# Turning the second expert place's rows by DMA transposes, in a gated-attention and expert-layer kernel

## The chip, the cores and the metric

The kernel runs on one core of a Trainium2 chip. The metric is the device time of one execution in microseconds. Three runs of the kernel before are shown; their median is 394.35 us. The engines of a core are called PE (matrix multiplications), DVE (vector), ACT (scalar), POOL (general) and SP (issues DMAs); 16 DMA engines move data for all of them.

## The reference

Two blocks follow each other. The first is a gated recurrent attention over sequences of 768 steps, the second a layer of 8 experts to which each of the 3072 rows is sent by the largest gate value.

```python
for t in range(S):                                   # 4 batches, 8 heads, width 48
    state = alpha[:, :, t, :, None] * state + np.einsum('bhd,bhe->bhde', k[:, :, t], v[:, :, t])
    y[:, :, t] = np.einsum('bhd,bhde->bhe', q[:, :, t], state)
x = y.transpose(0, 2, 1, 3).reshape(3072, 384)
logits = x @ w_gate                                  # (3072, 8)
expert_idx = np.argmax(logits, axis=1)
gate_w = softmax(logits)[row, expert_idx]
for e in range(8):
    rows = expert_idx == e
    out[rows] = gate_w[rows, None] * (np.maximum(x[rows] @ w1[e], 0.0) @ w2[e])
```

w1 is 384 x 1024 and w2 1024 x 384 for each expert, all in float32.

## The kernel before, in words

**Attention** takes the first 137 us or so. It works through 24 tiles of 128 rows, writes each row, scaled by its gate weight, to a buffer in DRAM (`x_d`), and finds out which rows go to which expert.

**Experts** follow as eight *places* (`groups`, `caps`). Place 0 is always expert 0, the others follow in order of how many rows an expert got. Place 1 has 416 rows, each later one 8 less. What does not fit is done by a loop after the places. For a place:

- `gather` (L372, POOL) fetches its rows from `x_d` by indirect DMAs, one for each block of 128 rows.
- The rows are *turned*, so that the width of 384 lies on the partitions: tile `xgT` (`g["xT"]`), one buffer.
- `row_sums` (DVE) makes five sums of halves of `xgT` in tile `t`, and `weight_sums` sums of halves of the weights in `s1` and `s2`. With these, places 1 to 7 do both layers by a scheme of seven products in place of eight (`chain`, `layer1`, `layer2`).
- The result `zT` is turned back and scattered to the output by POOL (`put`, L1078).

There are two ways to turn. `turn` (L855 on) has PE transpose each block of 128 x 128 against an identity into PSUM (L860), and DVE or ACT copy it to `xgT` (L861). `x_halves` (L866 on) splits a block of rows into its upper and lower 16-bit halves (L870, tile `xh`), has SP issue a DMA transpose for the block (L871, tile `xt`), and `x_whole` (L874 on) joins the halves to `xgT` on ACT (L878). Before the change, place 0 and place 1 are turned by `turn`, places 2 to 7 by the halves. Tile `xt` has one buffer, `xh` four.

**Place 0** is done in two parts. The 256 rows known early (`eg`) have layer one during the end of the attention, and layer two by `early_layer2` in two blocks j of 128 rows and eight pieces f (L1205, 2 matmul instructions to a piece). The *rest* of 168 rows is turned by `turn(g0)`, and then has `rest_layer1` (L1213 on): eight f, of which the even ones get their relu on ACT (L1228) and the odd ones on DVE (L1225). After each odd one a stretch of `places()` runs on DVE; that is the planning for the loop after the places, and it makes `xn`, which SP loads at L1343. `rest_layer2` (L1231 on) has three d of eight f (L1236), each with a copy to `zT` on ACT (L1239); its three results use the two banks of pair pA in turn.

**Order.** The program is written under a manual schedule (`tc.manual_schedule()`): each engine runs its instructions in the order of the program text, and an instruction that waits holds what stands behind it on its engine. So the generators (`l2`, `pl`, `between`) that are stepped with `next` are the order written out by hand. SP issues weight loads (`weights`, L179 and L182), the DMA transposes, and the writes of `x_d` in that order. Weights have two buffers for each layer, so `weights(i + 2, 1)` waits until place i has used its w1, while place 1's two loads find free buffers.

The order about the change, before it: layer two of early block 0 (eight pieces); gather of place 1; early block 1, pieces 0 to 3; `turn(g0)`; `rest_layer1`; early block 1, pieces 4 to 7, and its scatter; `weights(1, 2)`, `weights(2, 1)`; gather of place 2; the halves of place 2 on POOL; `turn(nxt)` of place 1 (first step of `turned()`); `ahead(1)`, the layer-one weight sums of place 1; `rest_layer2` d = 0; `row_sums` of place 1; d = 1 and 2; `weights(2, 2)`; then `layer1` of place 1 (L966).

Of the kernel before, what the change touches and what calls it, by code (L numbers as in the profile page):

```python
# [8 lines left out]
F32 = mybir.dt.float32  # L9
# [11 lines left out]
def kernel(  # L21
# [31 lines left out]
    C = 128  # L53
# [8 lines left out]
    DB = Dm // C  # L62
# [9 lines left out]
    NJ = 4  # L72
    SR = NJ * C
    CAP0, STEP = 424, 8
# [101 lines left out]
    def fetch(ex, layer):  # L176
        if layer == 1:
            w = wpool.tile([C, DB, F], F32, name="w1")
            nc.sync.dma_start(w[:], moe_w1[bass.ds(ex, 1)].rearrange("e (a p) f -> p (e a) f", p=C))  # L179
        else:  # L180
            w = wpool.tile([C, FB, Dm], F32, name="w2")
            nc.sync.dma_start(w[:], moe_w2[bass.ds(ex, 1)].rearrange("e (a p) d -> p (e a) d", p=C))  # L182
        return w
# [4 lines left out]
    FH = FB // 2  # L188
# [5 lines left out]
    def sub(eng, out, a, b):  # L194
        eng.tensor_tensor(out, a, b, op=ALU.subtract)  # L195
# [164 lines left out]
    def weights(i, layer):  # L360
        if 0 < i < E:
            ex = nc.sync.value_load(pd["xe"][0:1, i : i + 1], min_val=0, max_val=E - 1)
            groups[i][f"w{layer}"] = fetch(ex, layer)

    def blocks(g, by=1):
        return [(j, min(C, -(-(g["n"] - j * C) // by) * by)) for j in range(-(-g["n"] // C))]
# [22 lines left out]
    with tc.tile_pool(name="ld", bufs=6) as ld, \  # L389
         tc.tile_pool(name="work", bufs=2) as work:  # L390
        st = {s: {} for s in range(NT)}
        y = ps.tile([C, 2, 512], F32, name="y")
# [436 lines left out]
        _, s_e, gf_e, sf_e = next(d)  # L829
# [4 lines left out]
    wk = ctx.enter_context(tc.tile_pool(name="moe_wk", bufs=1))  # L834
# [4 lines left out]
    def bank(n):  # L839
        b = banks[n]  # L840
        if len(b) < 2:
            t = pairs[n][len(b)]
            if n == "y":
                b.append(y[:, t, :])
            else:
                b.append(ps.tile([C, 512], F32, name=t, bufs=2 if t == "tp" else 1)[:])
        else:
            b.append(b.pop(0))
        return b[-1]

    def blocks_of(t):
        return t[:, : DB * C].rearrange("p (a c) -> p a c", a=DB)


    def turn(g, *names):  # L855
        g["xT"] = wk.tile([C, DB, CAP0 + 8], F32, name="xgT")
        for j, r in blocks(g):
            tp = blocks_of(bank(names[j]))
            for a in range(DB):
                nc.tensor.transpose(tp[:, a, :r], g["xg"][:r, j, a * C : (a + 1) * C], ident[:r, :r])  # L860
            (nc.scalar.copy if j % 2 else nc.vector.tensor_copy)(g["xT"][:, :, j * C : j * C + r], tp[:, :, :r])  # L861
            if j == 1:
                yield

    def x_halves(g, copy=nc.scalar.copy):

        g["xt"] = wk.tile([C, NJ, 2 * DB, C], U16, name="xt")
        for j, r in blocks(g, 16):
            t = wk.tile([C, 2, Dm], U16, name="xh", bufs=4)
            copy(t[:r], g["xg"][:r, j, :].bitcast(U16).rearrange("p (c h) -> p h c", h=2))  # L870
            nc.sync.dma_start(g["xt"][:, j, :, :r], t[:r].rearrange("p h c -> p (h c)"), transpose=True)  # L871
            yield

    def x_whole(g):  # L874
        g["xT"] = wk.tile([C, DB, CAP0 + 8], F32, name="xgT")
        to = halves(g["xT"])
        for j, r in blocks(g):
            nc.scalar.copy(  # L878
                to[:, :, :, j * C : j * C + r], g["xt"][:, j].rearrange("p (h a) t -> p h a t", h=2)[:, :, :, :r],
            )  # L880

    def halves(t):
        return t.rearrange("p a t -> p (a t)").bitcast(U16).rearrange("p (a t h) -> p h a t", h=2, a=DB)

    def row_sums(g):
        m = g["n"] // 2
        g["t1"] = wk.tile([C, 5, CAP0 // 2 + 12], F32, name="t1")
        x, t = g["xT"], g["t1"][:, :, :m]
        h0, h1 = slice(0, m), slice(m, 2 * m)
        sub(nc.vector, t[:, 0], x[:, 0, h1], x[:, 0, h0])  # L890
        sub(nc.vector, t[:, 1], x[:, 1, h1], t[:, 0])
        sub(nc.vector, t[:, 2], x[:, 1, h1], x[:, 0, h1])
        sub(nc.vector, t[:, 3], x[:, 1, h0], t[:, 1])
        sub(nc.vector, t[:, 4], x[:, 2, h0], x[:, 2, h1])
# [305 lines left out]
    def early_layer2(j, fs):  # L1200

        if 0 in fs:
            eg["z"] = bank("y" if j else "pA")
        for f in fs:
            nc.tensor.matmul(  # L1205
                eg["z"][:, :Dm], lhsT=eg["h"][:, f, j * C : (j + 1) * C], rhs=groups[0]["w2"][:, f, :],
                start=(f == 0), stop=(f == FB - 1),
            )
        if FB - 1 in fs:
            yield  # L1210
            scatter(eg, j, C, eg["z"][:, :Dm])
        yield

    def rest_layer1(g, beside):
        n = g["n"]
        g["h"] = wk.tile([C, FB, CAP0], F32, name="h_sb")
        for f in range(FB):
            hp = bank("p" + "CBA"[f % 3])
            for a in range(DB):
                nc.tensor.matmul(  # L1220
                    hp[:, :n], lhsT=g["w1"][:, a, f * C : (f + 1) * C], rhs=g["xT"][:, a, :n],
                    start=(a == 0), stop=(a == DB - 1),
                )
            if f % 2:
                nc.vector.tensor_scalar_max(g["h"][:, f, :n], hp[:, :n], 0.0)  # L1225
                next(beside, None)
            else:
                nc.scalar.activation(g["h"][:, f, :n], hp[:, :n], AF.Relu)  # L1228

    def rest_layer2(g, d):  # L1230
        n = g["n"]  # L1231
# [12 lines left out]
    pl = places()  # L1244
# [2 lines left out]
        g["gi"], g["si"] = cols_of(gp, i * NJ), cols_of(sp, i * NJ)  # L1247
    gather(groups[1])
    next(l2)
    next(early_layer2(1, range(FH)))  # L1250
    for _ in turn(g0, "pC", "pC"):
        pass

    def beside(i):

        work = [z_halves(groups[i - 1])]
        if i == 1:
            work += [weight_sums(groups[1], 2, nc.vector)]
        while work:
            work = [w for w in work if next(w, w) is not w]  # L1260
            yield

    for i, g in enumerate(groups):
        nxt = groups[i + 1] if i + 1 < E else None
        rest = []

        last = i == E - 1

        def begin():
            if last:  # L1270
                rows_layer2(g, 0, ready)
            else:
                p1, tail = layer2(g)
                p1()
                rest.append(tail)

        if last:

            nc.gpsimd.drain()
        if i:  # L1280
            layer1(g, beside(i), begin, last)
        else:
            rest_layer1(g, pl)

            for _ in early_layer2(1, range(FH, FB)):
                pass
            weights(1, 2)
        weights(i + 2, 1)
        if i + 2 < E:
            gather(groups[i + 2])  # L1290
        if i == 0:
            for _ in x_halves(groups[2], nc.gpsimd.tensor_copy):
                pass

        def ahead(*layers):
            if nxt:
                for layer in layers:
                    for _ in weight_sums(nxt, layer, nc.vector):
                        pass

        def turned():
            if i == 0:
                for _ in turn(nxt, "pC", "pC", "y", "pB"):
                    pass
                yield
                row_sums(nxt)
                yield
            z_whole(groups[i - 1], nc.scalar.copy, 0, 1)
            yield
            if nxt:  # L1310
                row_sums(nxt)
            z_whole(groups[i - 1], nc.scalar.copy, 2)
            z_whole(groups[i - 1], nc.vector.tensor_copy, 3)
            yield
            if i + 2 < E:
                for _ in x_halves(groups[i + 2]):
                    pass
            yield

        between = turned()  # L1320

        if 0 < i < E - 1:
            x_whole(nxt)
        if last:
            for _ in between:
                pass
            for j, r in blocks(g):
                rows_layer2(g, j, (*([] if j == 0 else ready), FH - 1, FB - 1))
                scatter(g, j, r, g["z"][:r, :Dm], shared=j == NJ - 2)
        elif i:  # L1330
            rest[0](lambda: ahead(*((1,) if i == E - 2 else (1, 2))), between)
        else:
            next(between)
            ahead(1)
            rest_layer2(g, 0)
            next(between)
            rest_layer2(g, 1)
            rest_layer2(g, 2)
        weights(i + 2, 2)
# [4 lines left out]
    with tc.If(nx > 0):  # L1344
        with tc.For_i(0, nx, 1) as i:
# [13 lines left out]
            g = dict(n=C, w1=fetch(ex, 1), w2=fetch(ex, 2), gi=lambda j, r: gi[:, 0:1], si=lambda j, r: si[:, 0:1], apart=False)  # L1359
# [32 lines left out]
```

## Time and profile before

| | |
|---|---|
| three runs, median | 394.35 us |
| the profiled execution's own time | 394.27 us |
| its span, first to last instruction | 392.5 us |
| busy: PE / DVE / ACT / POOL | 382.1 / 211.6 / 225.5 / 149.7 us |
| mean granted clock of PE | 0.999 |
| rest's layer one, first matmul (L1220) | 156.91 us |
| rest's layer two, first matmul (L1236) | 167.91 us |
| place 1's layer one, first matmul (L966) | 174.85 us |

Times are in us from the first instruction of the profiled execution. In a timeline, a line has start, length, engine, line of the kernel, operation, output <- input, number of instructions merged, and in brackets how long the engine was idle ahead of it and what released it. The ends of matmuls are modelled, so that lengths of neighbours overlap; starts are the firmer figure. PEld are the weight loads of PE, which run beside its matmuls. SPq is the queue of SP: the length of a DMA there is the time that issuing took, and the time to landing is told apart from it.

### The profile page before, as it was taken

How to read it: one execution, taken by the hardware profiler on the slowest of the kernel's cores; microseconds unless marked ns; L12 is line 12 of the kernel's file. 1: busy time of each engine (PE TensorE's matmuls, PEld its weight loads, DVE VectorE, ACT ScalarE, POOL GpSimd, SP SyncE). 2: the span in 40 equal slices, each digit the busy share in tenths (PEclk: the TensorE clock that was granted, in tenths of full speed). 3: DMA queues.
4: the chain of work that ended last, by engine and by line, in shares of the span. 5: the costliest groups of instructions: out<-in, count | busy, mean ns of one | idle time of the engine just before them, and what ended most of it. 6: DMA issues, size and time to landing. Idle time of an engine off the chain costs nothing.

```text
span 392.5 us, 9105 instructions
## 1 busy us (share of the span) xinstructions
PE 382.1 (97%) x3390; PEld 325.6 (83%) x3390; DVE 211.6 (54%) x651; ACT 225.5 (57%) x515; POOL 149.7 (38%) x203
## 2 busy tenths in 40 slices
PE   6999999999999999999999999999999999999994
PEld 4678888888888785899889979979979979979852
DVE  5554667676675566455853572582581681552200
ACT  5476677777655441126664776675665765673540
POOL 6646564789768204184051034025026012021041
PEclk9999999999999999999999999999999999999999
DMA  9999998999996215768939659658668766600321
GB/s 172 204 182 231 189 223 188 226 201 220 236 224 178 96 42 216 256 227 236 158 137 260 77 202 206 177 187 216 169 200 193 187 201 150 172 21 36 60 72 42
DMA packets 153921, 67.44 MB, mean 172 GB/s; under 512 B 136715, under 2 KB 148098, under 8 KB 153876
## 3 DMA queue, kind: packets, MB, share of 16 engines
q1 hardware_dynamic: 148772, 57.13, 60.8%
q0 software_dynamic: 3408, 9.64, 8.0%
q8 instruction: 27, 0.44, 0.5%
q10 hardware_dynamic: 1696, 0.08, 0.3%
q14 instruction: 18, 0.15, 0.1%
HBM read 49.00 MB, written 9.58 MB: 149 GB/s over the span
## 4 chain that ended last, share of the span: by engine, by line
PE 78%; issue 15%; POOL 2%; ACT 2%; DVE 1%; DMA 1%; POOLq 0%; ACTq 0%; DVEq 0%
PE tp L1048 7%; PE tp L489 6%; PE sA L502 6%; PE y L539 5%; PE x L966 4%; PE sA L966 4%; PE x L576 4%; PE sA L1031 4%; PE tp L966 3%; PE sB L966 3%; PE cum L966 3%; PE x L1031 3%; PE y L529 3%; PE cum L430 2%; PE tp L1031 2%
## 5 line engine op out<-in xcount | busy, mean ns | idle before, releaser
L1078 POOL DMA_INDIRECT out_dram<-zo,sp x25 | 26.1, 1042 | 137.5 <-ACT zo L1103 127.0
L479 POOL TENSOR_TENSOR kqb<-k_sb,icp 128x384 f32<-128x384 f32 x23 | 23.0, 1001 | 29.6 <-PE y L550 12.4
L1048 PE MATMUL tp<-h_sb,w 128*128 128x416 f32 (+5 forms) x96 | 33.9, 496 | 0.0
L502 PE MATMUL sA<-qT,kT 48*128 48x128 f32 x192 | 27.7, 284 | 0.9 <-DVE qT L493 0.9
L372 POOL DMA_INDIRECT xg<-x_rows,gp x25 | 24.0, 962 | 10.0 <-issue 6.5
L502 PE MATMUL sB<-qT,kT 48*128 48x128 f32 x192 | 27.7, 285 | 0.0
L489 PE MATMUL tp<-ident,kqb 128*128 128x128 f32 x192 | 26.2, 279 | 0.6 <-DVE kqb L479 0.6
L1048 PEld LDWEIGHTS tp<-h_sb,w 128*128 128x128 f32 x96 | 18.0, 190 | 10.3 <-issue 3.7
L502 PEld LDWEIGHTS sA<-qT,kT 48*128 48x128 f32 x192 | 23.1, 187 | 3.8 <-ACT kT L495 1.1
L192 DVE TENSOR_TENSOR h_sb<-sB,u 128x208 f32<-128x208 f32 (+6 forms) x28 | 10.1, 360 | 27.3 <-PE sB L966 20.8
L977 ACT ACTIVATE h_sb<-h_sb 128x208 f32<-128x208 f32 (+6 forms) x28 | 10.2, 366 | 25.2 <-DVE h_sb L192 25.2
L479 POOL TENSOR_TENSOR kqb<-q_sb,cp 128x384 f32<-128x384 f32 x23 | 23.1, 1004 | 2.8 <-DMA q_sb<-in_q_dram 2.3
L192 DVE TENSOR_TENSOR h_sb<-cum,u 128x208 f32<-128x208 f32 (+6 forms) x28 | 10.1, 360 | 26.1 <-PE cum L966 18.7
L489 PEld LDWEIGHTS tp<-ident,kqb 128*128 128x128 f32 x192 | 20.5, 140 | 3.4 <-issue 1.2
L558 ACT COPY yT<-y 128x512 f32<-128x512 f32 x24 | 14.1, 587 | 16.0 <-PE y L550 10.3
L966 PE MATMUL tp<-xgT,w 128*128 128x208 f32 (+6 forms) x112 | 23.1, 329 | 0.0
L502 PEld LDWEIGHTS sB<-qT,kT 48*128 48x128 f32 x192 | 23.1, 187 | 0.0
L510 DVE TENSOR_TENSOR dA<-sA,cmask 128x512 f32<-128x512 f32 x24 | 16.5, 689 | 11.2 <-PE sB L502 11.0
L195 DVE TENSOR_TENSOR th<-h_sb,th 128x208 f32<-128x208 f32 (+5 forms) x48 | 17.4, 362 | 7.9 <-ACT h_sb L979 7.9
L576 PE MATMUL x<-iw,yT 128*64 128x104 f32 x368 | 20.8, 255 | 0.1
L1103 ACT COPY zo<-zr 128x768 uint16<-128x768 uint16 (+2 forms) x20 | 20.0, 1052 | 0.0
L966 PEld LDWEIGHTS tp<-xgT,w 128*128 128x128 f32 x112 | 19.3, 190 | 0.0
(308 smaller groups left out, 1030.4 us busy)
## 6 DMA issues: line engine op xcount, KB each, us to landing
w<-in_moe_w_dram SPq DMA_DIRECT2D x14, 1536.0 KB, 6.9
x_rows<-xs SPq DMA_DIRECT2D x24, 192.0 KB, 3.6
v_sb<-in_v_dram SPq DMA_DIRECT2D x10, 384.0 KB, 4.8
k_sb<-in_k_dram SPq DMA_DIRECT2D x9, 384.0 KB, 6.7
q_sb<-in_q_dram SPq DMA_DIRECT2D x9, 384.0 KB, 6.0
a_sb<-in_alpha_dram SPq DMA_DIRECT2D x7, 384.0 KB, 4.5
a_sb<-in_alpha_dram SPq DMA_DIRECT2D x10, 192.0 KB, 3.7
w<-in_moe_w_dram SPq DMA_DIRECT2D x6, 256.0 KB, 3.5
```

Of the source, the lines that this page charges most:

```text
L192: eng.tensor_tensor(out, a, b, op=ALU.add)
L372: nc.gpsimd.indirect_dma_start(out=g["xg"][:r, j, :], out_offset=None, in_=x_d[:, :], in_offset=bass.IndirectOffsetOnAxis(ap=g["gi"](j, r) ...
L479: eng.tensor_tensor(by_half(kq[:, i]), d[n].rearrange("s (a p) d -> s a p d", a=2), d[e][:].rearrange("s (a p d) -> s a p d", a=2, p=NP), ...
L489: nc.tensor.transpose(tp[:, p, :], pair(kqb[s % 3][:, i], p), ident[:])
L502: nc.tensor.matmul(t[:, p, :], lhsT=d["kT"][r : r + D, p, :], rhs=d["qT"][r : r + D, p, :], start=True, stop=True,)
L539: nc.tensor.matmul(yv(g)[o : o + D, j, :], lhsT=d["v"][:, g * NP + p, :], rhs=d["d" + "AB"[g]][:, p, :], start=(s < B and j == 0), stop=Tr ...
L576: nc.tensor.matmul(d["x"][o : o + HC, m, : D2 + E], lhsT=d["yT"][:, m // 2, m % 2, o : o + HC], rhs=iw[:, m, :], start=True, stop=True,)
L966: nc.tensor.matmul(out, lhsT=ops[n_][0], rhs=ops[n_][1], start=first and n_ == names[0], stop=True, skip_group_check=True,)
L1031: nc.tensor.matmul(out, lhsT=lhs, rhs=rhs, start=first and f == 0, stop=True, skip_group_check=True)
L1048: nc.tensor.matmul(d2[:, :n], lhsT=w2[:, f, 2 * C :], rhs=h[:, f, :n], start=(f == 0), stop=(f == FB - 1),)
L1078: ins = nc.gpsimd.indirect_dma_start(out=out[:, :], out_offset=bass.IndirectOffsetOnAxis(ap=g["si"](j, r), axis=0), in_=zo[:r], in_offset= ...
L1103: copy(zo[:r].bitcast(U16).rearrange("p (c h) -> p h c", h=2), g["zr"][:r, j].rearrange("p (h a) c -> p h (a c)", h=2),)
```

## The change

Place 1's rows are no longer turned by PE. Their four blocks are split on ACT, one after each even f of `rest_layer1`, and SP issues a DMA transpose after each. The joins stand on ACT behind `rest_layer1`: blocks 0 and 1 ahead of the early block's last four pieces, blocks 2 and 3 behind them. `weights(1, 2)`, whose place in the text stays the same, thereby stands behind the four transposes on SP. `row_sums` of place 1 is called directly, at the place of the second step of `turned()`. Besides, piece 3 of early block 1 moves from before the rest's turning to behind it.

```diff
-    def x_whole(g):
-        g["xT"] = wk.tile([C, DB, CAP0 + 8], F32, name="xgT")
+    def x_whole(g, *js):
+        if 0 in js:
+            g["xT"] = wk.tile([C, DB, CAP0 + 8], F32, name="xgT")
         to = halves(g["xT"])
         for j, r in blocks(g):
+            if j not in js:
+                continue
             nc.scalar.copy(
...
-    def rest_layer1(g, beside):
+    def rest_layer1(g, beside, rows):
...
                 nc.scalar.activation(g["h"][:, f, :n], hp[:, :n], AF.Relu)
+                next(rows)
...
-    next(early_layer2(1, range(FH)))
+    next(early_layer2(1, range(FH - 1)))
     for _ in turn(g0, "pC", "pC"):
         pass
+    next(early_layer2(1, (FH - 1,)))
...
-            rest_layer1(g, pl)
-
+            rest_layer1(g, pl, x_halves(nxt))
+
+            x_whole(nxt, 0, 1)
             for _ in early_layer2(1, range(FH, FB)):
                 pass
+            x_whole(nxt, 2, 3)
             weights(1, 2)
...
         def turned():
-            if i == 0:
-                for _ in turn(nxt, "pC", "pC", "y", "pB"):
-                    pass
-                yield
-                row_sums(nxt)
-                yield
             z_whole(groups[i - 1], nc.scalar.copy, 0, 1)
...
-            x_whole(nxt)
+            x_whole(nxt, *range(NJ))
...
-            next(between)
             ahead(1)
             rest_layer2(g, 0)
-            next(between)
+            row_sums(nxt)
             rest_layer2(g, 1)
             rest_layer2(g, 2)
```

## The prediction

> **What bounds the kernel now.** I read the page first, then the PE timeline of the place where the change sits, then ACT and SP there. Page, sections 1 and 4:
>
> ```profile
> span 392.5 us, 9105 instructions
> ...
> PE 382.1 (97%) x3390; PEld 325.6 (83%) x3390; DVE 211.6 (54%) x651; ACT 225.5 (57%) x515; POOL 149.7 (38%) x203
> ...
> PE 78%; issue 15%; POOL 2%; ACT 2%; DVE 1%; DMA 1%; POOLq 0%; ACTq 0%; DVEq 0%
> ```
>
> PE is busy for 97% of the span and the chain that ended last runs through it. So an instruction taken from PE shortens the run, as long as no operand comes late. The timeline of PE around the change (start, length, instructions):
>
> ```profile
> 153.14 2.74 PE L1205 MATMUL y<-w,h 128*128 128x384 f32 x8
> 155.72 0.80 PE L860 MATMUL tp<-ident,xg 128*128 128x128 f32 x6
> 156.91 1.09 PE L1220 MATMUL tp<-xgT,w 128*128 128x168 f32 x6 [0.39 <-ACT xgT L861]
> ...
> 163.82 2.74 PE L1205 MATMUL y<-w,h 128*128 128x384 f32 x8
> 166.40 0.82 PE L860 MATMUL tp<-ident,xg 128*128 128x128 f32 x6
> 167.14 0.55 PE L860 MATMUL y<-ident,xg 128*128 128x128 f32 x3
> 167.62 0.37 PE L860 MATMUL sB<-ident,xg 32*128 32x32 f32 x3
> 167.91 2.55 PE L1236 MATMUL x<-h_sb,w 128*128 128x168 f32 x16
> 170.29 2.44 PE L1236 MATMUL sA<-h_sb,w 128*128 128x168 f32 x16
> ```
>
> Two things cost PE time. At 156.91 it sits idle for 0.39 us until ACT has copied the rest's second turned block. From 166.40 to 167.91 it turns the second place's rows (L860, 12 instructions). Everything else is back to back; the waits of PE after 150 us are this one and one of 0.3 us at the end.
>
> The machinery that takes over exists for later places. The view of tile xt (durations min/median/max in ns):
>
> ```profile
> L871 SPq DMA_TRANSPOSE xt<-xh x21: 1173/1279/2250, 174.4 to 328.1; - x21
> L878 ACT COPY xgT<-xt x21: 233/1042/1051, 193.3 to 346.5; 128x768 uint16<-128x768 uint16 x16, 128x144 uint16<-128x144 uint16 x1, 128x96 uint16<-128x96 uint16 x1, 128x48 uint16<-128x48 uint16 x1
> ...
> DMA to landing us min/median/max: 3.6/4.1/5.2
> ```
>
> And one line of who SP's queue waited for:
>
> ```profile
> SPq L1343 <- DVE xn L1177: 8.3, 1, 8.3
> ```
>
> A transpose holds SP's issue for 1.28 us and lands 4.1 us after it. Splitting a block (L870, in the view of tile xh) takes ACT 0.83 us, joining it (L878) 1.04 us, the block of 32 rows some 0.25.
>
> **What the Trainium skill says.** "TensorE: Matmul & The Clock Gate", Part 4 (PE-mode transpose): a PE transpose ends in PSUM and needs a copy after it, some 275 ns in one kernel. The trace agrees: 273 ns a piece (pipelined 0.13 apart), with copies at L861. "DMA: Bandwidth & Descriptors", DMA Transpose (X-bar): the DMA transpose takes 2-byte types only and is issued from SP or ACT; that is why rows are split into uint16 halves. Same page, Queues, rings and completion order: one issuer's descriptors are consumed in ring order. The trace agrees: the z transpose issued at 181.80 behind a 1.5 MB weight load of 180.91 landed 9.7 us later, against 4.0 for the rows' transposes at 176 to 178 without a load ahead of them.
>
> **The change part by part.**
>
> *Moved piece.* One f of early layer two is 2 of 8 instructions, 2.58/8 x 2 = 0.645 us. Moved behind the rest's turning, the turning starts at 155.07 and its PE part ends at 155.87. The last copy, which ended at 156.82, ends 0.65 earlier, so L1220 could start at 156.26; the piece runs from 155.87 to 156.52. It covers the whole wait: 0.39 saved. It issues no DMA. The rest's rows must be there at 155.07: the two gathers issued at 148.00 and 149.29 land 2.9 and 2.7 us later, by 152.
>
> *Turning taken off PE.* 167.91 - 166.40 = 1.51. The first L1236 group lasts 167.91 to 170.29 = 2.38, the next 170.29 to 172.57 = 2.28: 0.10 for the switch after transposes goes too. The 4 copies out of PSUM (1.96 us together on DVE and ACT) go from engines with slack.
>
> *Sum:* 0.39 + 1.51 + 0.10 = 2.00 us, if nothing comes late. The profiled execution took 394.27 (its span 392.54 and 1.7 around it): 392.27. The median of the three runs shown is 394.35, 0.08 above it: **392.35**.
>
> *Added on ACT, four splits.* One follows each relu at f = 0, 2, 4, 6. ACT is idle 1.4 us between these relus, 0.31 + 0.83 fits. Each waits for its gather. These were issued at 153.59, 154.86, 156.11 and 157.37 and landed 5.9, 6.2, 6.3, 5.4 later, while 3 MB of weights moved; group 2's took 3.2 to 2.6. The early end is 156.8, 158.0, 159.1, 160.0, the late end 159.5, 161.1, 162.4, 162.8. Behind a waiting split stands the next relu. At the late end the splits end at 160.3, 161.9, 163.2 and 164.4 and the f = 6 relu at 163.6. PE reads that h only in rest_layer2, from 166.0, so even this end costs nothing; PE's banks are six, so f = 6 and 7 reuse those of f = 0 and 1, freed earlier. With the early end the splits end at 158.8, 160.5, 162.2, 163.9. I expect something near it, since layer two's weights now move later.
>
> *Added on SP, four transposes.* Issued after each split, the last at 164.0 (early) or 164.5 (late); landing + 4.1: 168.1 to 168.6. A bound from below is 3.6, from above 9.7 (that z transpose).
>
> *Joins on ACT.* Blocks 0 and 1 at 164 to 166 (early), then the early scatter's copy, then blocks 2 and 3. The last (0.25) ends at 168.4 to 169.0. Behind it on ACT stands the zT copy of rest_layer2's first d, whose matmuls end at 163.43 + 2.58 + 2.4 = 168.4. PE needs that bank again at the third d: 163.43 + 2.58 + 2.28 x 2 = 170.6. So there are 1.3 to 1.9 us of cover, and a landing after 170.0 starts to cost, us for us.
>
> *row_sums* moves behind the joins: 1.63 us on DVE (170.80 to 172.43 now), so 168.7 to 170.6. Layer one of place 1 starts at 172.85 and reads t 1.06 later, at 173.9: cover 3 us. The sums of layer one's weights no longer wait for the turning's copies.
>
> *Moved on SP.* weights(1, 2), 1.5 MB, issued at 151.76 now, stands behind the four transposes: 165.8. weights(2, 1) waits for w1's buffer in both, 164.02 now, and follows at some 166.5; group 2's transposes come behind both. Alone a load takes 6.9 to land (the view of issues at 150.5), so w2 lands by 173, and w1 by 177, since both share one ring. The first user of w2 is DVE's sum at 179.31, 177.3 after the shift: cover 4 us. Without it, DVE's queue (the h additions) stops and PE behind it. w1 of place 2 is first summed at 194.57: covered. POOL's gathers for group 2 (168.67 on) meet these loads: landing at 6 instead of 3 delays POOL's splits by 3 us, their transposes and weights(2, 2) on SP likewise; their reader is the join at 193.30: covered.
>
> **Rivals.** (1) *Part is given back*: SP's load of xn (L1343, which waits till 161.3) comes ahead of the transposes. Nothing in the diff places it; now it sits where SP has nothing else to do. Then the transposes issue at 161.4, 162.7, 164.0, 165.3 and the last lands at 169.4 to 170.5: 0 to 0.8 us of stall at the third d. With somewhat slow transposes up to 1.5: 392.7 to 393.8. (2) *Slower*: the last transpose lands as late as the z transposes did, 164.0 + 9.7 = 173.7. ACT then stands in the join, the zT copy behind it ends at 174.25, and PE waits at the third d from 170.6: 3.65 lost, 394.35 - 2.00 + 3.65 = 396.0. It ends above before once the landing is later than 172.0. Against it: those had a weight load ahead in the ring, and these have theirs behind. (3) *The turning was hidden anyway*, the end set by a DMA: then 394.3. Against it: PE runs without such waits from here to 387 us. (4) *More than the sum*, 390.8 to 391.7, if a later hand-over closes as well; nothing in the views names one.
>
> **How the numbers follow.** The sum as it stands, 391.8 to 392.8: 0.72. (1) 0.13, (2) 0.07, (3) 0.05, (4) 0.03. The range 391.7 to 394.1 takes in the sum, (1), and some of (3), with 0.2 for the scatter of the runs. Every case lies within 2% (7.9 us, about what a measurement of this kernel can tell from no change): the largest gain is 3.5 and the loss of (2) 1.7. So 0.96 within, 0.01 faster, 0.03 slower for a stall that I haven't seen.
>
> **What would show it.** PE: one L1205 group of 2 instructions between L860 and L1220 with no wait; L1236 straight behind L1205; no L860 at 166; layer one of place 1 at 172.9 instead of 174.85. ACT: four L870 copies between relus. SP: four L871 from 159 to 165, landing near 4. Wrong if PE waits at the third L1236 group for an ACT zT copy, if DVE's sum of w2 waits for a DMA, or if place 1's first matmuls wait for xgT or t.

## The result, and the profile after

| | before | after |
|---|---|---|
| median of 20 runs each, side by side | 394.49 us | 392.37 us |
| ratio after / before, 95% interval | | 0.9946 [0.9935, 0.9957] |
| profiled execution, own time / span | 394.27 / 392.5 us | 391.55 / 389.8 us |
| first matmul of early block 0's layer two | 147.98 us | 147.56 us |
| first matmul of the rest's layer one | 156.91 us | 156.14 us |
| first matmul of the rest's layer two | 167.91 us | 165.56 us |
| first matmul of place 1's layer one | 174.85 us | 172.40 us |
| first matmul of place 2's layer one | 206.52 us | 204.06 us |

The kernel became 2.1 us faster (0.54%, interval 1.7 to 2.6 us); 392.35 was predicted. That 392.35 and 392.37 lie so close is luck: the base was taken 0.14 us too low (394.35 from three runs, 394.49 from twenty) and the gain 0.12 too small. One run of the 20 on each side took far longer (986.99 and 1474.76 us) and stays out of the ratio, and one profile below, that of the first kernel that turns place 0's rest by DMA, is of an execution at a granted clock of 0.989 and a span of 397.1 us, so only its waits are read.

The landmarks say where the time went, once a difference is taken between neighbours, so that the start of each execution drops out. From early block 0 to the rest's layer one PE took 8.93 us before and 8.57 after: 0.36 less. From there to the rest's layer two 11.00 and 9.42: 1.58 less. From there to place 1 6.94 and 6.84: 0.10 less. Place 1 itself took 31.66 in both, and every later place the same within 0.03. So the change gave 2.04 us between 148 and 175 us, and hardly anything (0.03) was handed back behind it. The spans differ by 2.72; of the other 0.7 us, 0.42 arose in the attention before the change's place and 0.29 behind the last matmul, where neither kernel differs. Over the profiles of this study early block 0 starts anywhere from 147.5 to 149.5 us, so the 0.42 is the scatter of executions.

The page of the kernel after, section 1, shows PE's busy time 2.0 us shorter and ACT's 4.7 us longer:

```profile
span 389.8 us, 9094 instructions
...
PE 380.1 (98%) x3378; PEld 324.1 (83%) x3378; DVE 210.0 (54%) x649; ACT 230.2 (59%) x521; POOL 149.2 (38%) x203
```

The PE timeline of the kernel after, about the change:

```profile
154.66 0.80 PE L860 MATMUL tp<-ident,xg 128*128 128x128 f32 x6
155.39 0.91 PE L1208 MATMUL y<-w,h 128*128 128x384 f32 x2
156.14 1.02 PE L1223 MATMUL tp<-xgT,w 128*128 128x168 f32 x6
...
162.98 2.74 PE L1208 MATMUL y<-w,h 128*128 128x384 f32 x8
165.56 2.44 PE L1240 MATMUL x<-h_sb,w 128*128 128x168 f32 x16
167.84 2.44 PE L1240 MATMUL sA<-h_sb,w 128*128 128x168 f32 x16
170.12 2.44 PE L1240 MATMUL x<-h_sb,w 128*128 128x168 f32 x16
172.40 0.52 PE L969 MATMUL sA<-xgT,w 128*128 128x208 f32 x2
```

No bracket is left: the two instructions of the moved piece (L1208) fill what was a wait of 0.39, L860 is gone behind the early block, and the first group of L1240 takes 2.28 us to the next, as the others do, where it took 2.38 behind the transposes. The only wait that the view of PE's waits still names from 140 us on is one of 0.3 us at the end (L1120).

ACT of the kernel after, with the splits (L870), the joins (L881) and the first copy to `zT`:

```profile
157.19 0.31 ACT L1231 ACTIVATE h_sb<-tp 128x168 f32<-128x168 f32 x1 [1.44 <-PE tp L1223]
157.40 0.82 ACT L870 COPY xh<-xg 128x768 uint16<-128x768 uint16 x1
...
163.72 1.98 ACT L881 COPY xgT<-xt 128x768 uint16<-128x768 uint16 x2 [0.38 <-DMA xt<-xh]
165.76 0.48 ACT L1077 COPY zo<-y 128x384 f32<-128x384 f32 x1
166.13 1.32 ACT L881 COPY xgT<-xt 128x768 uint16<-128x768 uint16 x2
168.04 0.30 ACT L1243 COPY zT<-x 128x168 f32<-128x168 f32 x1 [0.58 <-PE x L1240]
```

The last line is the one to read: the copy to `zT` waited for its matmuls, not for the joins ahead of it, which had ended at 167.45. And SP's queue with the view of tile `xt` over the whole run:

```profile
158.30 6.78 SPq L871 DMA_TRANSPOSE xt<-xh  x4
165.91 0.43 SPq L182 DMA_DIRECT2D w<-in_moe_w_dram  x1
167.50 0.38 SPq L179 DMA_DIRECT2D w<-in_moe_w_dram  x1
```
```profile
L871 SPq DMA_TRANSPOSE xt<-xh x25: 1174/1275/1842, 158.3 to 325.4; - x25
...
DMA to landing us min/median/max: 3.2/4.0/5.3
```

The four transposes are issued from 158.30 to 165.08, the weights of layer two (L182) and then those of place 2's layer one (L179) behind them.

### The profile page after: what moved, and what is told of

Read it like the earlier page. It is cut to its first block, busy times and chain, and to the rows that moved or that the text cites. A ratio compares the mean times of both kernels' runs of the same rounds, so it can differ in the third digit from the quotient of the medians.

```text
span 389.8 us, 9094 instructions
## 1 busy us (share of the span) xinstructions
PE 380.1 (98%) x3378; PEld 324.1 (83%) x3378; DVE 210.0 (54%) x649; ACT 230.2 (59%) x521; POOL 149.2 (38%) x203
## 4 chain that ended last, share of the span: by engine, by line
PE 77%; issue 15%; POOL 2%; DMA 2%; ACT 1%; DVE 1%; POOLq 0%; SPq 0%; ACTq 0%; DVEq 0%
PE tp L1051 7%; PE tp L489 6%; PE y L539 6%; PE sA L502 6%; PE x L969 4%; PE sA L969 4%; PE x L576 4%; PE sA L1034 4%; PE tp L969 3%; PE cum L969 3%; PE sB L969 3%; PE y L529 3%; PE x L1034 3%; PE tp L1034 2%; POOL out_dram L1081 2%
## 5 line engine op out<-in xcount | busy, mean ns | idle before, releaser
L881 ACT COPY xgT<-xt 128x768 uint16<-128x768 uint16 (+6 forms) x25 | 20.8, 925 | 0.4 <-DMA xt<-xh 0.4
```

Source lines behind the costliest of these rows:

```text
L881: nc.scalar.copy(to[:, :, :, j * C : j * C + r], g["xt"][:, j].rearrange("p (h a) t -> p h a t", h=2)[:, :, :, :r],)
```

## The experiments

All ratios are against the kernel before on the same chip, with 95% intervals. PE's landmarks are compared as above, between neighbours.

### Each part alone

The moved piece without the turning:

```diff
-    next(early_layer2(1, range(FH)))
+    next(early_layer2(1, range(FH - 1)))
     for _ in turn(g0, "pC", "pC"):
         pass
+    next(early_layer2(1, (FH - 1,)))
```

> The kernel before with the moved piece alone (one f of early block 1 behind the rest's turning). Theory of the sum: the wait of 0.39 us ahead of the rest's layer one is gone and nothing else changes: 0.39 us faster, ratio 0.999, place 1's first matmul 0.39 us earlier against the end of early block 0. Rival (the gain lies in the order of the DMAs or in the turning alone): no gain, ratio 1.000, a wait of the same length elsewhere.

Measured: 0.9996 [0.9986, 1.0007]. The expected 0.999 lies inside, and so does no change: inconclusive as a time. The trace is plain. PE took 8.57 us from early block 0 to the rest's layer one (8.93 before), 6.94 from the rest's layer two to place 1 (as before), and its view of waits no longer has the wait of 0.39.

The turning without the moved piece (the change with this edit):

```diff
-    next(early_layer2(1, range(FH - 1)))
+    next(early_layer2(1, range(FH)))
     for _ in turn(g0, "pC", "pC"):
         pass
-    next(early_layer2(1, (FH - 1,)))
```

> The changed kernel with the piece moved back ahead of the rest's turning: place 1 is turned by DMA transposes, the wait of PE ahead of the rest's layer one stays. Theory of the sum: 1.51 us of PE transposes and 0.10 us of the switch behind them are gone: 1.6 us faster than before, ratio 0.996; a wait of 0.3 to 0.4 us at the rest's first matmul. Rival (the turning was hidden anyway): ratio 0.999 or above.

Measured: 0.9982 [0.9972, 0.9992], that is 0.7 us of the 1.6 expected. The landmarks about the change are as they should be (8.93, 9.50, 6.84), but place 1 took 33.71 us in place of 31.66: PE stopped twice there, for 0.8 us at its start and for 1.1 us near 188, each time waiting for a copy on ACT (L911). Neither stop occurs in the change's own profile. So the same kernel was run again, beside the unaltered change:

> The changed kernel itself, unedited, beside the runs that follow on the same chip, because the turning alone came out 0.7 us faster and not 1.6, and with the early load of w2 no faster, both on another chip than the changed kernel. Theory of the sum: 2.0 us faster than before here too, ratio 0.995. Rival (the gain depends on the chip, some of it is lost to stops of place 1 that the profiles of that session show and the first profile of the change doesn't): ratio 0.997 to 0.998 here, with stops in place 1.

> The changed kernel with the piece moved back, as in the turning alone, now on the same chip as the changed kernel. Theory of the sum: 0.39 us slower than the changed kernel, ratio to before 0.996, a wait of 0.39 us ahead of the rest's layer one and the same times from there on. Rival (without the piece the transposes come at a worse moment and lose another microsecond in place 1): 1 us or more slower than the changed kernel.

Measured: the change 0.9937 [0.9919, 0.9956], the turning alone 0.9943 [0.9924, 0.9962]. Place 1 took 31.66 us in both profiles, without stops. The turning alone therefore gives its share (the 0.996 expected lies inside its interval). The shortfall of its first run goes with stops that come on some chips or in some executions: the profiled one, which was 1.0 us above the median of that run, lost 2.05 us in place 1. They turn up again below. The piece's own worth, 0.0006 between the two, can't be told from nothing in time. In the trace it can. The PE timeline of the turning alone has the wait back:

```profile
156.29 0.80 PE L860 MATMUL tp<-ident,xg 128*128 128x128 f32 x6
157.48 1.09 PE L1223 MATMUL tp<-xgT,w 128*128 128x168 f32 x6 [0.39 <-ACT xgT L861]
```

### How much cover the joins have

The change with four more joins of a block that is already joined, so that the data stay the same and ACT reaches the first copy to `zT` later:

```diff
             for _ in early_layer2(1, range(FH, FB)):
                 pass
+            for _ in range(4):
+                x_whole(nxt, 1)
             x_whole(nxt, 2, 3)
```

> The changed kernel with the join of block 1 done four times more on ACT (the same values written again, 4.2 us) ahead of the joins of blocks 2 and 3. It does what a landing 4.2 us later would do to ACT. Theory: joins end at 171.6 in place of 167.45, the zT copy of the first d ends at 171.9 in place of 168.3, and PE, which wants that bank at 170.1, waits 1.8 us there: the gain of 2 us is all but gone, ratio to before 0.999 to 1.000, and PE's wait is named after ACT zT. Rival (PE waits for xgT or t at place 1 instead, or not at all): no wait at the third d; the time of the changed kernel, or a loss that shows at place 1's first matmuls.

Measured: 0.9996 [0.9979, 1.0012]. PE now waits at the third d, and for the copy that the prediction named:

```profile
171.78 2.55 PE L1240 MATMUL x<-h_sb,w 128*128 128x168 f32 x16 [1.53 <-ACT zT L1243]
```

From the rest's layer two to place 1 it took 8.64 us, 1.80 more than the change; place 1 lost another 0.69 in two short stops. On this chip the turning alone had lost 0.9 us without any added joins, so the time by itself would prove little; the wait does. Counted from early block 0, the joins ended 4.15 us later than in the change and PE lost 1.80, so the change has some 2.3 us of cover here. So ACT's queue is where lateness would reach PE, through the bank that the first and the third d share, and in the change it doesn't: that copy waits for PE.

### The order of the weights on SP

Layer two's weights last, behind place 2's layer-one weights (an edit of the change):

```diff
             x_whole(nxt, 2, 3)
-            weights(1, 2)
         weights(i + 2, 1)
+        if i == 0:
+            weights(1, 2)
```

> The changed kernel with the loads of place 2's w1 and place 1's w2 issued in the other order, so that w2 has 3 MB ahead of its end in the ring instead of 1.5. It lands at about 177 instead of 173. Theory (cover of 4 us): DVE's first sum of w2, at 176.85 in the changed kernel, waits 0.5 us or less, the additions behind it come late by as much, and the run is 0 to 0.5 us longer than the changed kernel. Rival (the loads are far from any use): no wait at all and the same time. Rival (w2 is on the path): more than 1 us longer.

Measured: 0.9968 [0.9955, 0.9980]; 393.32 us, against 392.46 for the change on the same chip. Place 1 took 32.38 us, 0.72 more. The DVE line of its first sum of these weights:

```profile
179.76 0.69 DVE L192 TENSOR_TENSOR s<-w 128x512 f32<-128x512 f32 x1 [2.48 <-DMA w<-in_moe_w_dram]
```

The load was issued at 167.82 and landed near 179.7, where the change's sum starts at 176.85 and waits for nothing. DVE's h additions stand behind the sum, and PE behind them. The cover of layer two's weights is real and finite, and the second of the two loads landed some 12 us after its issue.

Layer two's weights first, ahead of the transposes, as the kernel before had them:

```diff
         else:
+            weights(1, 2)
             rest_layer1(g, pl, x_halves(nxt))
...
             x_whole(nxt, 2, 3)
-            weights(1, 2)
```

> The changed kernel with the load of place 1's w2 (1.5 MB) issued ahead of the four transposes, as early as before. Theory (cover): gathers land some 6 us after their issue as before, the splits come up to 0.5 us later, the transposes run behind the load in the ring, the last lands at about 168 to 169, joins end before 170.1 in the changed kernel's times, so the time is that of the changed kernel within 0.3 us. Rival 2 of the prediction (a transpose near a weight load lands 9.7 us after its issue): the last lands at 171 to 174, ACT stands in the join, PE waits 1 to 3.5 us at the third d of the rest's layer two, and the run is 1 to 3.5 us longer than the changed kernel.

Measured: 0.9995 [0.9977, 1.0013]: nothing is left of the gain. The theory that was put on record for a second run was that the stops of the first were chance:

> The changed kernel with place 1's w2 issued ahead of the four transposes, once more, because in the session of its first run the turning alone too came out 1.4 us longer than beside the changed kernel later, and the stops in its profile stood in place 1 and not where the cover ends. Theory (cover): the joins end some 2 us later than in the changed kernel but before the third d wants its bank: ratio to before 0.994 to 0.996, no wait at the third d. Rival (the early load costs what the change gains): 0.998 or more.

Measured: 0.9996 [0.9981, 1.0011]. That theory fell: both times the kernel with this order is no faster than the kernel before. It isn't the cost that I would have guessed, a late turning. In both profiles the joins end before PE's third d, PE doesn't wait there, and the landmarks up to place 1 are the change's (8.57, 9.42, 6.84). The loss of the profiled executions stands in place 1, which took 32.97 and 33.47 us, and nearly all of it at its start (1.31 and 1.58 us). It differs from one execution to the next: the 22 of the first run took 392.6 to 398.3 us, those of the kernel before beside them 393.6 to 396.7. PE and ACT of the second run:

```profile
173.57 0.87 PE L969 MATMUL tp<-xgT,w 128*128 128x208 f32 x4
176.13 0.62 PE L969 MATMUL sA<-t,s 128*128 128x208 f32 x2 [1.69 <-ACT p L911]
```
```profile
171.14 0.30 ACT L1243 COPY zT<-sA 128x168 f32<-128x168 f32 x1 [1.23 <-PE sA L1240]
175.02 0.30 ACT L1243 COPY zT<-x 128x168 f32<-128x168 f32 x1 [3.58 <-PE tp L969]
```

The copy at 175.02 reads what PE's third d had finished by 173.4, and ACT was idle. What it lacked was PE's report: the semaphore that PE counts up for this matmul group is recorded at 175.00 us, and the next two, due at 173.7 and 174.4, at 175.73 and 175.78. In the change's profile no such report from 147 us on comes more than 0.03 us after its modelled end.

The early load can't be the only cause of such a stop. The first profile of the turning alone, whose order of loads is the change's, has the same one: the report of the third d, due at 174.03, is recorded at 175.24, and the copy starts at 175.26. And the change itself has no run known to be on the three chips on which this order was run. On the first of them the turning alone was short by 0.9 us too; by the medians (394.78 against 394.13, and 0.44 for the piece) the order's own share there is estimated at 1.1 us. On the other two the versions with both turnings by DMA (below), which load these weights behind the transposes, kept the whole gain, but they differ in more than this order. How much of the loss is the order's is therefore not shown.

When that report came, at 175.00, POOL had just issued the last of the four gathers of place 2 (169.8 to 174.5), beside the load of place 2's layer-one weights. Hence the next experiment, an edit of this kernel, which moves those gathers ahead of the early block's scatter on POOL:

```diff
-            for _ in early_layer2(1, range(FH, FB)):
-                pass
+            late = early_layer2(1, range(FH, FB))
+            next(late)
+            gather(groups[2])
+            next(late)
             x_whole(nxt, 2, 3)
...
-        if i + 2 < E:
+        if 0 < i < E - 2:
             gather(groups[i + 2])
```

> The kernel of the run before with w2's load ahead of the transposes, with one more edit: POOL issues the gathers of place 2 ahead of the early block's scatter instead of behind it, so at some 160 to 165 us, beside w2's load, instead of 170 to 174.5, beside w1's. Theory (the 1.3 to 1.8 us that place 1 loses at its start, from 173.4 on, come from the four gathers meeting the 1.5 MB load of w1 just then): the stops go, place 1 takes 31.7 us again instead of 33.0 to 33.5, and the ratio to before is 0.994 to 0.996. Rival (they come from the load of w1 alone at the start of place 1, or from something else that w2's earlier place brings): place 1 still takes 32.9 to 33.5 us and the ratio stays at 0.999 to 1.000. If the gathers beside w2's load hold back the transposes of place 1, PE waits at the third d, and the profile shows that apart from place 1.

Measured: 0.9997 [0.9983, 1.0012]. Neither theory has it. Place 1 took 31.91 us, so the stop at its start went, as the first one said; but the time didn't follow, because the stop came earlier instead, where the gathers now were (issued from 159.8 to 164.5). ACT and the PE view of waits:

```profile
160.79 0.83 ACT L870 COPY xh<-xg 128x768 uint16<-128x768 uint16 x1 [0.56 <-DMA xg<-x_rows,gp]
166.44 0.32 ACT L1231 ACTIVATE h_sb<-sB 128x168 f32<-128x168 f32 x1 [4.81 <-PE y L1208]
```
```profile
PE x L1240 <- ACT zT L1243: 0.7, 1, 0.7
```

The relu at 166.44 reads a bank that PE's matmuls had filled by 160.9, so ACT stood 4.8 us; the third split and transpose, which are queued behind that relu, came 5 us late. From the rest's layer two to place 1 PE took 8.48 us, 1.64 more than the change: 0.69 of it within the first d, and 0.95 at the third, where the copy to `zT` waited behind the late joins.

### The rest of place 0 turned by DMA too

If PE's turning was worth its own time, the other turning (L860 for the rest) should be worth about 0.8 us as well. This version (against the change) loads place 1's layer-one weights behind the rest's transposes:

```diff
-        weights(1, 1)
...
     g0["si"] = cols_of(s_e, EARLY // C)
+    for _ in x_halves(g0):
+        pass
+    weights(1, 1)
...
-    next(early_layer2(1, range(FH - 1)))
-    for _ in turn(g0, "pC", "pC"):
+    x_whole(g0, 0, 1)
+    for _ in early_layer2(1, range(FB)):
         pass
-    next(early_layer2(1, (FH - 1,)))
...
             x_whole(nxt, 0, 1)
-            for _ in early_layer2(1, range(FH, FB)):
-                pass
-            x_whole(nxt, 2, 3)
...
             rest_layer2(g, 0)
+            x_whole(nxt, 2, 3)
             row_sums(nxt)
```

> The changed kernel with the rest of place 0 turned by DMA transposes as well: its two blocks are split on ACT as soon as its gathers land, w1 of place 1 is loaded behind these two transposes, all eight pieces of early block 1 run on PE ahead of the rest's layer one, and the joins of place 1's blocks 2 and 3 stand behind the first d of the rest's layer two. Theory: the 0.73 us of PE transposes for the rest go and nothing comes late (its joins end near 157.4, the rest's layer one starts at 157.9): 0.7 us faster than the changed kernel, ratio to before 0.993. Rival (the rest's rows come late, or place 1's joins, now without early pieces between, do): a wait ahead of the rest's layer one or at place 1, and no gain or a loss up to 1 us.

Measured: 0.9989 [0.9966, 1.0011]. The rest's layer one started without a wait, but in the profiled execution, of 398.79 us, the rows of place 1 came late, and PE waited 4.4 us where the second rival of the prediction has it:

```profile
PE x L1239 <- ACT zT L1242: 4.4, 1, 4.4
```

In the usual execution the wait can't have been as long: 12 of the 22 took 392.2 to 393.6 us, which leaves no room for 4.4 us on top of the 392.46 of the change. Its gathers of place 2 had moved forward too, to 161.5 us, since the scatter that holds them on POOL came sooner. The next version keeps the early block's copy and scatter behind the first two joins:

```diff
     x_whole(g0, 0, 1)
-    for _ in early_layer2(1, range(FB)):
-        pass
+    late = early_layer2(1, range(FB))
+    next(late)
...
             x_whole(nxt, 0, 1)
+            next(late)
             weights(1, 2)
```

> The rest of place 0 turned by DMA too, as before, with the copy and scatter of early block 1 put behind the joins of place 1's blocks 0 and 1, so that POOL comes to the gathers of place 2 at 167 again and not at 161.5, where they shared the DMA engines with place 1's transposes. Theory (those gathers, and w1 of place 1 just ahead in the ring, made the transposes late): place 1's transposes land earlier, the wait for zT at the third d shrinks to 1 us or less, ratio 0.991 to 0.995. Rival (w1 of place 1, now loaded 6 us later, alone makes them late): the wait stays, ratio 0.997 or more.

> The kernel with the rest of place 0 turned by DMA as well and the early block's copy and scatter behind the first two joins, once more with more rounds. It takes 1.03 us more off PE (9 transposes of the rest, 0.80, and the gaps about them) than the change and keeps 0.07 of a wait at the third d. If that is worth what the trace of its first run shows (0.50 us from early block 0 to place 1 against the change's trace), the ratio is 0.9930 to 0.9937, some 0.0010 to 0.0015 below the change's 0.9937 to 0.9946. If the transposes of two places crowd SP and the rows of place 1 come late in most executions, the ratio is 0.996 or more.

Measured: 0.9928 [0.9905, 0.9952] and, again, 0.9932 [0.9915, 0.9948]. Neither interval meets that of the version before, so the place of the early block's copy and scatter, and with it that of the gathers of place 2, was worth some 2 us, as the theory of the run had it. The PE timeline of the first has no L860 left:

```profile
153.82 5.32 PE L1207 MATMUL y<-w,h 128*128 128x384 f32 x16
158.98 1.02 PE L1222 MATMUL tp<-xgT,w 128*128 128x168 f32 x6
```

From early block 0 to the rest's layer two PE took 17.16 us in both, 0.83 less than in the change. But it gave 0.33 and 0.68 of that back from there to place 1 (in the second, 0.4 waiting at the third d for the copy to `zT`), and the second lost 0.65 inside place 1. So from early block 0 to place 2 the profiled execution of the first took 0.5 us less than the change's and that of the second 0.5 more. In time both stand below the change's 0.9937 and 0.9946, but the intervals overlap: that this version is better is not shown.

## Why the prediction was right, step by step

*The sum.* It said 2.00 us; the landmarks show 2.04, the times 2.1. By term: moved piece 0.39 predicted, 0.44 measured (0.36 for the wait, and 0.08 since the group behind it no longer starts from a standstill: 1.02 us in place of 1.09; alone it shows 0.36 and 0.07); turning off PE 1.51 predicted, 1.50 in the turning alone; the switch behind transposes 0.10 and 0.10. All three could be read from the PE timeline of before, because PE there ran without gaps up to its end. A microsecond taken from it was then a microsecond of the run, as long as nothing new came late, and the rest of the prediction was about that.

*Splits on ACT.* The early end was right: they ended at 158.2, 159.9, 161.6 and 163.3 (158.8 to 163.9 predicted, with all times 0.4 later in that profile), and none waited for its gather. The gathers landed 2.5 to 3.8 us after their issue, against 5.4 to 6.3 before. As the prediction argued, layer two's weights are no longer under way then. The other order shows it: with those weights ahead again, three splits waited, 1.8, 0.6 and 0.3 us in the second run.

*Transposes on SP.* The last was issued at 163.84 (164.0 predicted). The first join waited 0.38 us for a landing, the later ones not at all. The joins ended at 167.45, where 168.4 to 169.0 was predicted, less the 0.42 by which this execution ran ahead. The term that was mis-sized is the last landing. By the semaphore updates in the trace the four landed 5.3, 4.3, 2.8 and 2.4 us after their issue, the last at 166.26; it was priced at 4.1, with 3.6 as the bound from below. That the last block holds only 32 rows can't be the whole reason, since the third, a full block, took 2.8; what made the first two slower was not tested. The cover was thus larger than the 1.3 to 1.9 us said: some 2.3, as the added joins measure it.

*The first rival* had SP's load of `xn` ahead of the transposes. It came between the second and the third, at 161.7, and moved the third and fourth by at most 0.9 us, inside the cover. *The second rival*, a landing too late for the third d, did not occur; but its path to PE is real: with joins 4.2 us later PE lost 1.80 us at that place, and 4.4 in the profile of the first version with two turnings by DMA. *The third*, a turning hidden anyway, is excluded by the turning alone (0.9943). *More than the sum* found nothing: every later place takes the same time.

*row_sums* ran from 167.48 to 169.1; PE reads `t` at 173.45, 4.3 us of cover where 3 were said.

*Weights.* The load of layer two's weights was issued at 165.91, landed at 173.87, and the first sum at 176.85 didn't wait. The cover was 3.0 us where 4 were said, since the load took 8.0 us to land and not 6.9; that it is finite shows from the other side, where the load behind the other one cost 0.7 to 0.9 us. And "w1 lands by 177" was too early: that load, the second in line, was issued at 167.50 and landed at 178.97, 11.5 us later, with four gathers under way beside it. It cost nothing because place 2's weights are first summed at 192.1. The gathers of place 2 met these loads as predicted, and the splits on POOL waited for them:

```profile
174.87 0.82 POOL L870 COPY xh<-xg 128x768 uint16<-128x768 uint16 x1 [2.33 <-DMA xg<-x_rows,gp]
```

No reader on PE's path saw that: place 2 and the later places took the same time as before.

*What the prediction didn't see* is the stops. It costed the place of `weights(1, 2)` as a matter of cover; with that load ahead of the transposes the whole gain was missing in three runs of two kernels, in two of the three profiles with no late landing that cost PE anything. How much of that is the order's and how much the chips' is open. In the two profiles of the change itself there is no such stop, and that the prediction held there is in part good fortune: on the chip where the turning alone first ran, its share of the sum came out at less than half.

## What to carry to other kernels

Where the bounding engine has no gaps, price a removed instruction at its full time, and spend the care on what the removal newly depends on: find the one instruction in the new helper's queue that the bounding engine reads next (here the first copy to `zT`), and compute its slack. An experiment that adds known work ahead of it measures this slack at once. Here it came to some 2.3 us, where the prediction had 1.3 to 1.9. When a step is moved, the loads queued behind it move too, and their order has to be priced and tried as well: layer two's weights as the last of the loads cost 0.9 us on the same chip, and as the first of them the gain was missing on each of three chips, for a reason that is not settled.

## What was unexpected of the hardware

The stops. In some executions an engine stands for 1 to 5 us because another engine's report comes late, while that engine's own instructions go on. With layer two's weights loaded ahead of the transposes, PE's report of a group that ended at 173.4 us came at 175.00; with the gathers moved, the relu of a group that ended at 160.9 started at 166.44. In that stretch of the latter kernel SP, too, took 0.7 us over an instruction that takes 0.02 elsewhere. When the gathers of place 2 were moved 10 us forward, the stop moved with them. But gathers beside a weight load are not enough: the change has them as well, from 167.8 to 172.5, and no such stop in either of its profiles.

Nor is the early load needed: the first run of the turning alone has the stop without it. What causes it stays open. The traces of the kernels run on three of the chips lack some of the semaphore updates (in the second run with layer two's weights ahead, 922 are recorded of some 980 that PE, ACT and DVE made after 138 us), also in places where nothing was held up, so a missing update proves no stop; the starts of the waiting instructions do. The chip alone doesn't explain it: the versions with both turnings by DMA ran on two of these chips with traces of that kind and kept the whole gain, while the turning alone lost more than half of it on the third and nothing on a chip with complete traces. The order with layer two's weights ahead was run only on the three chips and the change itself, as far as is known, only on others. So whether that order costs 2 us elsewhere, and whether the change gains 2 us there, is not known.
